# One x tile turned by DMA instead of TensorE, its loads behind it, the k-v copies first, five more stores at the end

## The chip, the cores and the metric

The kernel runs on one core of a Trainium2 chip. The metric is the device time of one execution in microseconds, as a median of several. Runs of the kernel before lie within 0.35 us of each other in any one set of rounds, about 0.1%. The second tool is the trace: the distances between the same two instructions on TensorE in two runs agree to some hundredths of a microsecond where nothing waits.

"Tile 6" below is the seventh group of 128 rows of x, counted from zero; "batch index 2" is the third of the eight batches. Group one is the second group of four tiles (4 to 7), group two the tiles 8 to 11. The prediction and the expectations count groups from one, so their "group two" is group one, and their "group three" is group two.

In the lines of the profile PE is TensorE, PEld its weight loads, DVE VectorE, ACT ScalarE, POOL GpSimd; a q behind a name (SPq) means that the engine's sequencer issues a DMA. L513 is line 513 of the kernel, and `out<-in` names the buffers written and read: xT is the turned x, raw_k the loaded k, ob an output tile on its way out. A line of a timeline gives start, length, what, and in brackets how long the engine was idle before and what ended that. The chain is the work that ended last, followed back from the end of the program; it shows start, length and what. A DMA "lands" when its completion semaphore has its full count.

## The reference, cut to what matters

```python
def _attn_ref(q, k, v):                      # batch 8, heads 8, rows 576, width 64
    q_p, k_p = phi(q, cos_w, sin_w), phi(k, cos_w, sin_w)     # relu, times cos and sin: width 128
    kv = np.einsum('bhsf,bhsd->bhfd', k_p, v)
    z = np.sum(k_p, axis=2)
    return np.einsum('bhsf,bhfd->bhsd', q_p, kv) / (np.einsum('bhsf,bhf->bhs', q_p, z)[..., None] + 1e-06)

def _moe_ref(x, w_gate, w_val, w_out):       # x: 4608 rows of 512, inner width 1536
    g = x @ w_gate
    return (g * (1.0 / (1.0 + np.exp(-g))) * (x @ w_val)) @ w_out
```

The result of the attention, rearranged to 4608 x 512, is the x of the second part.

## The kernel before

Nine groups of four x tiles go through the feed-forward part. While TensorE works on one group, the attention of the next is threaded into it: `at(step, ...)` puts small pieces of work behind the steps of the running group. A group has twelve steps of gate and value products (`ffn_fc`) and four output tiles (`ffn_out`); group zero's output is cut into twelve steps named (0, 0) to (2, 3).

A tile of x must be turned before the products can take it. There are two ways:

```python
def x_turn(t, fast=False):
    if fast:
        x_turn_pe(t)              # four transposes on TensorE, into PSUM
        x_turned(t, "act")        # a copy to xT on ScalarE
    else:
        nc.sync.dma_start_transpose(out=xT_of(t), in_=st["x", t])
```

The first product of a group takes all four tiles at once, so it waits for the last of the four turns:

```python
nc.tensor.matmul(out=..., lhsT=(wg_sb, wv_sb)[i][:, kc, fs], rhs=xT[tg][:, ts, kc], ...)   # L513
```

Loads of k and v are issued by GpSimd. To keep one back, the kernel lets GpSimd read two elements of something that a DMA writes:

```python
def load_2():
    nc.gpsimd.tensor_copy(out=hold2, in_=xT[1][0:1, 0, 0, 0:2])    # waits for tile 4's turn
    for nm in ("k", "v"):
        load(2, nm)

at((0, 1), turn(4), load_2)
at((1, 0), turn(5), a_(6, 0))
at((1, 1), a_(6, 1))
...
at((2, 0), turn(6, True))
at((2, 2), turn(7, True))
```

`load_3` does the same for batch index 3, held by tile 10. Where q of the second batch is turned, TensorE, ScalarE and VectorE meet:

```python
at("b11", lambda: kv_mm(1), q_(1, 0, 0), q_(1, 1, 0, "dve"), lambda: kv_out(1))
at((0, 0), lambda: kv_free(1), a_(4, 0), a_(4, 1))
```

`kv_mm` makes the k-v products, `q_` turns q on TensorE and copies it out (to phit), `kv_out` copies the k-v products out (to kvd), and `a_` multiplies the two. "b11" is the last product step of group zero.

## Time and profile before

| | before |
|---|---|
| time, median of 3 | 325.12 us |
| span in the trace | 323.2 us |
| TensorE busy | 316.1 us, 98% |
| VectorE, ScalarE, GpSimd busy | 56%, 40%, 11% |
| tile 5's transpose by DMA, issue to landing | 2.4 us |
| tile 10's, which holds the load of index 3 | 2.5 us |

With TensorE at 98% the question for any change is what TensorE no longer has to do, or no longer waits for. Busy time is not enough for that, since a wait of some tenths disappears in it; the start of the instruction behind the wait is the thing to read. The lines themselves are in the prediction.

### The profile page before, as it was taken

The page shows a single profiled execution, that of the slowest core. Times are in us where ns is not written, and L with a number is a line of the kernel's source. Part 1 is how long each engine was busy: PE and PEld are TensorE (multiplying, and loading weights), DVE is VectorE, ACT ScalarE, POOL GpSimd, SP SyncE. Part 2 cuts the span into 40 slices and gives each one's busy share as a digit, 9 for nine tenths or more (in the row PEclk, how much of TensorE's full clock was granted, in tenths as well). Part 3 has the DMA queues.
Part 4 walks back from the last instruction along what each step waited for, and adds up shares of the span by engine and source line. Part 5 has one row for each costly group of instructions (what it writes and reads, how often), then busy time and mean ns, then how long its engine had stood idle before and what let it go on. Part 6 is the DMA issues. An engine that isn't in the chain of part 4 may idle for free.

```text
span 323.2 us, 6031 instructions
## 1 busy us (share of the span) xinstructions
PE 316.1 (98%) x2384; PEld 159.0 (49%) x2384; DVE 180.9 (56%) x363; ACT 130.7 (40%) x239; POOL 35.3 (11%) x60
## 2 busy tenths in 40 slices
PE   7899999999999999999999999999999999999995
PEld 3596555454445444544454445444544444444443
DVE  7873766787448747564756555755573236323320
ACT  7553546662436345333533354335432132213311
POOL 6755002010101000110011000200000000000000
PEclk9999999999999999999999999999999999999999
DMA  7999997987995988599679968895912401240014
GB/s 267 215 200 197 206 194 136 213 113 108 178 200 79 184 152 134 79 175 177 116 97 160 164 123 118 134 184 109 134 36 48 103 14 35 50 103 11 0 32 97
DMA packets 74379, 41.01 MB, mean 127 GB/s; under 512 B 49904, under 2 KB 69104, under 8 KB 74352
## 3 DMA queue, kind: packets, MB, share of 16 engines
q1 hardware_dynamic: 52000, 22.95, 38.9%
q0 software_dynamic: 22192, 17.57, 36.6%
q8 instruction: 18, 0.29, 0.4%
q10 hardware_dynamic: 160, 0.13, 0.1%
q14 instruction: 9, 0.07, 0.1%
HBM read 37.75 MB, written 9.44 MB: 146 GB/s over the span
## 4 chain that ended last, share of the span: by engine, by line
PE 95%; ACT 2%; DVE 2%; issue 0%; ACTq 0%
PE banks L513 58%; PE banks L549 28%; PE banks L285 3%; PE banks L399 2%; PE banks L444 1%; PE banks L381 1%; DVE v L239 1%; PE banks L152 1%; PE banks L568 1%; PE banks L325 0%; PE banks L485 0%; ACT L184 0%; ACT phit L333 0%; PE banks L274 0%; ACT ob L571 0%; DVE qwT L369 0%
## 5 line engine op out<-in xcount | busy, mean ns | idle before, releaser
L524 DVE TENSOR_TENSOR ht<-sg,banks 128x512 bf16<-128x512 bf16 (+2 forms) x116 | 74.7, 650 | 68.7 <-PE banks L513 60.3
L513 PE MATMUL banks<-xT,wv_sb 128*128 128x512 bf16 (+2 forms) x464 | 111.3, 364 | 0.0
L513 PE MATMUL banks<-xT,wg_sb 128*128 128x512 bf16 (+2 forms) x464 | 111.3, 364 | 0.0
L519 ACT ACTIVATE sg<-banks 128x512 bf16<-128x512 f32 (+2 forms) x116 | 65.8, 568 | 111.6 <-PE banks L513 107.7
L549 PE MATMUL banks<-wo_sb,ht 128*128 128x512 bf16 x420 | 93.8, 379 | 0.0
L513 PEld LDWEIGHTS <-wv_sb 128*128 128x128 bf16 x464 | 44.8, 98 | 48.7
L513 PEld LDWEIGHTS <-wg_sb 128*128 128x128 bf16 x464 | 43.1, 98 | 42.8
L549 PEld LDWEIGHTS <-ht 128*128 128x128 bf16 x420 | 40.3, 98 | 45.7 <-issue 0.2
L556 ACT COPY ob<-banks 128x512 f32<-128x512 f32 x18 | 10.6, 586 | 54.0 <-PE banks L549 54.0
L235 DVE TENSOR_TENSOR r_q<-raw_q,tab 128x1152 bf16<-128x1152 bf16 x24 | 17.9, 754 | 20.7 <-ACT raw_q L218 20.7
L556 DVE COPY ob<-banks 128x512 f32<-128x512 f32 x17 | 11.7, 691 | 28.6 <-PE banks L549 28.6
L239 DVE TENSOR_TENSOR v<-raw_v,tab 128x1152 bf16<-128x1152 bf16 x31 | 22.8, 753 | 0.1
L421 DVE TENSOR_TENSOR x<-banks,rec 128x512 bf16<-128x512 f32 (+1 forms) x32 | 21.6, 674 | 1.3 <-PE banks L381 0.3
L218 ACT ACTIVATE raw_k<-raw_k 128x576 bf16<-128x576 bf16 (+1 forms) x25 | 17.1, 694 | 0.0
L218 ACT ACTIVATE raw_q<-raw_q 128x576 bf16<-128x576 bf16 x24 | 15.5, 679 | 0.0
L729 POOL COPY hold<-phit 1x2 bf16<-1x2 bf16 x5 | 0.9, 175 | 129.6 <-DMA phit<-r_q 129.6
L399 PEld LDWEIGHTS <-phit 128*128 128x128 bf16 (+1 forms) x240 | 10.0, 100 | 6.5 <-issue 1.3
L399 PE MATMUL banks<-kv,phit 128*128 128x65 bf16 (+1 forms) x240 | 11.6, 195 | 0.0
L152 PE MATMUL banks<-zeros 128*128 128x64 bf16 (+1 forms) x64 | 8.5, 292 | 1.0 <-DVE zeros L147 1.0
L308 DVE CAST kv<-banks 64x260 bf16<-64x260 f32 x12 | 5.1, 428 | 7.4 <-ACT kv L308 7.3
L285 PEld LDWEIGHTS <-raw_k 64*64 64x64 bf16 x504 | 7.6, 106 | 3.0 <-issue 2.1
L285 PE MATMUL banks<-v,raw_k 64*64 64x130 bf16 x504 | 8.8, 218 | 0.0
(84 smaller groups left out, 130.9 us busy)
## 6 DMA issues: line engine op xcount, KB each, us to landing
out_dram<-ob SPq DMA_DIRECT2D x70, 128.0 KB, 2.4
raw_k<-in_k_dram POOLq DMA_DIRECT2D x7, 576.0 KB, 9.1
raw_q<-in_q_dram POOLq DMA_DIRECT2D x6, 576.0 KB, 6.3
raw_v<-in_v_dram POOLq DMA_DIRECT2D x6, 576.0 KB, 12.0
wo_sb<-in_moe_w_out_dram POOLq DMA_DIRECT2D x3, 512.0 KB, 13.0
wg_sb<-in_moe_w_gate_dram POOLq DMA_DIRECT2D x5, 256.0 KB, 8.6
wv_sb<-in_moe_w_val_dram POOLq DMA_DIRECT2D x5, 256.0 KB, 9.2
wo_sb<-in_v_dram SPq DMA_DIRECT2D x2, 576.0 KB, 4.3
```

Of the source, the lines that this page charges most:

```text
L152: nc.tensor.matmul(out=ps, lhsT=zeros, rhs=zeros[:, 0:cols].unsqueeze(1).to_broadcast([P, 4, cols]), start=True, stop=True)
L218: nc.scalar.activation(out=out, in_=in_, func=AF.Relu)
L235: nc.vector.tensor_tensor(out=st[b, "q"][:, g], in0=o.unsqueeze(2).to_broadcast([P, NC, 2, D]), in1=tab, op=ALU.mult)
L239: nc.vector.tensor_tensor(out=v2s[b % 2][:, g, :, :, 0:D], in0=(first if b == 0 and g == 0 else {"v": raw_of(b, "v")})["v"][:, g].unsqueez ...
L285: nc.tensor.matmul(out=ps[i * D:(i + 1) * D, e, j * 2 * D1:(j + 1) * 2 * D1], lhsT=raws[b, "k"][es, g, c], rhs=v2s[b % 2][es, g, c, :, 0:D ...
L399: nc.tensor.matmul(out=ps[ms, e, g * D1:(g + 1) * D1], lhsT=phit[b][:, e, g, c:c + n].rearrange("p c s -> p (c s)"), rhs=kv2s[b % 2][:, e, ...
L421: nc.vector.tensor_tensor(out=st["x", t].rearrange("p (y e d) -> p e y d", e=2, d=D)[:, :, ys], in0=ps[:, :, 0:2 * J * D1].rearrange("p e ...
L513: nc.tensor.matmul(out=st["f", tg, fc, lo][i], lhsT=(wg_sb, wv_sb)[i][:, kc, fs], rhs=xT[tg][:, ts, kc], start=(kc == 0), stop=(kc == KC - 1))
L519: nc.scalar.activation(out=sg[:, 0:n], in_=st["f", tg, fc, lo][0], func=AF.Silu)
L524: nc.vector.tensor_tensor(out=hts[tg % 2][:, fc, r:r + n], in0=st.pop(("s", tg, fc, lo))[:, 0:n], in1=ps[1], op=ALU.mult)
L549: nc.tensor.matmul(out=o_ps[t], lhsT=hts[tg % 2][:, fc, r:r + P], rhs=wo_sb[:, fc], start=(fc == 0), stop=(fc == FC - 1))
L556: (nc.scalar.copy if t % 2 == 0 else nc.vector.tensor_copy)(out=ob, in_=ps)
```

## The change

Its intent: take four transposes and a copy off the engines, remove a small wait for kvd, give the loads and the attention of batches index 2 and 3 one more step of room, and arrange the last stores differently. Its core, with cuts marked:

```diff
-            nc.sync.dma_start(out=out_v[...], in_=ob[e * SH:(e + 1) * SH])
+            parts = 2 if NH - 9 <= idx < NH - 4 else 1
+            for i in range(parts):
+                cols = slice(i * d_model // parts, (i + 1) * d_model // parts)
+                nc.sync.dma_start(out=out_v[...][:, cols], in_=ob[e * SH:(e + 1) * SH, cols])
...
-                (nc.sync if e else nc.scalar).dma_start(out=out_v[...][:, lo:hi],
+                (nc.scalar if e else nc.sync).dma_start(out=out_v[...][:, lo:hi],
...
-    at("b11", lambda: kv_mm(1), q_(1, 0, 0), q_(1, 1, 0, "dve"), lambda: kv_out(1))
+    at("b11", lambda: kv_mm(1), lambda: kv_out(1), q_(1, 0, 0), q_(1, 1, 0, "dve"))
...
-        nc.gpsimd.tensor_copy(out=hold2, in_=xT[1][0:1, 0, 0, 0:2])
+        nc.gpsimd.tensor_copy(out=hold2, in_=xT[1][0:1, 1, 0, 0:2])
...
-    at((0, 1), turn(4), load_2)
+    at((0, 1), turn(4))
...
-    at((1, 1), a_(6, 1))
+    at((1, 1), a_(6, 1), turn(6), load_2)
...
-    at((2, 0), turn(6, True))
...                                  (k, v and q work of index 2 and 3: one step later each)
-            at((9, 10, 11)[i - 1] + SLOTS, lambda t=t: a_tile2(t), turn(t))
+            at((10, 11, 12)[i - 1] + SLOTS, lambda t=t: a_tile2(t), turn(t))
             if i == 2:
-                at(11 + SLOTS, load_3)
+                at(12 + SLOTS, load_3)
```

More of the change, by code (lines that the diff above doesn't have):

```diff
@@ L558, in ffn_out @@
             idx = 2 * t + e
-            nc.sync.dma_start(out=out_v[idx // NC, idx % NC], in_=ob[e * SH:(e + 1) * SH])
+            parts = 2 if NH - 9 <= idx < NH - 4 else 1
+            for i in range(parts):
+                cols = slice(i * d_model // parts, (i + 1) * d_model // parts)
+                nc.sync.dma_start(out=out_v[idx // NC, idx % NC][:, cols], in_=ob[e * SH:(e + 1) * SH, cols])
     def ffn_out_last(t):
@@ L573, in ffn_out_last @@
                 idx = 2 * t + e
-                (nc.sync if e else nc.scalar).dma_start(out=out_v[idx // NC, idx % NC][:, lo:hi],
+                (nc.scalar if e else nc.sync).dma_start(out=out_v[idx // NC, idx % NC][:, lo:hi],
                                                         in_=ob[e * SH:(e + 1) * SH, 0:hi - lo])
@@ L749 @@
         if b == 2:
-            fs, tq = [s0 + i for i in (0, 0, 1, 1, 4, 5, 5, 6)], (s0 + 2, s0 + 2)
+            fs, tq = [s0 + i for i in (0, 0, 1, 1, 5, 6, 6, 7)], (s0 + 4, s0 + 4)
         else:
@@ L754 @@
             if b == 3:
-                fs, tq = [p0 + 12 + i for i in range(4)] + [s0 + 4, s0 + 4, s0 + 5, s0 + 5], (s0 + 2, s0 + 2)
-            at(p0 + 3 if b < 5 else p0 + 1, lambda b=b: load_behind(b))
-        tk = (s0 + 4, s0 + {2: 8, 3: 7}.get(b, 5))
+                fs, tq = [p0 + 13 + i for i in range(4)] + [s0 + 5, s0 + 5, s0 + 6, s0 + 7], (s0 + 3, s0 + 3)
+            at(p0 + 4 if b < 5 else p0 + 1, lambda b=b: load_behind(b))
+        tk = (s0 + 4, s0 + {2: 9, 3: 8}.get(b, 5))
         for s, f in zip(fs, steps):
```

## The prediction

> **What bounds the kernel now.** I read the page first: the busy shares and the slices, then the chain that ended last.
>
> ```profile
> PE 316.1 (98%) x2384; PEld 159.0 (49%) x2384; DVE 180.9 (56%) x363; ACT 130.7 (40%) x239; POOL 35.3 (11%) x60
> ...
> PE   7899999999999999999999999999999999999995
> ...
> DMA  7999997987995988599679968895912401240014
> ...
> PE 95%; ACT 2%; DVE 2%; issue 0%; ACTq 0%
> ```
>
> TensorE is busy for 316.1 of 323.2 us, and the only slices of the forty under 9 are the first two and the last. The chain is 95% PE. So time comes out of this kernel only where TensorE issues less, or where it waits: at the head (not touched by the change), at the tail, and in small waits inside the slices that print as 9.
>
> A busy digit can hide such waits, because ends of matmuls are modelled. So I read the chain in order of time from 34 to 60 us, the stretch that most of the change touches; start, length, what:
>
> ```profile
> 38.88 1.27 PE banks L285 x69
> 40.15 0.51 PE banks L274 x7
> 40.66 0.02 issue
> 40.69 0.91 ACT phit L333
> 41.59 0.27 ACT kvd L297
> 41.87 0.01 issue
> 41.88 0.38 ACT kvd L297
> 42.26 0.04 issue
> 42.30 0.72 PE banks L444 x7
> ...
> 51.42 0.22 PE banks L485 x4
> 51.64 0.86 PE banks L549 x4
> ```
>
> Two things are to be seen. From 40.69 to 42.30 the chain leaves PE: ScalarE first copies the turned q (phit, 0.91 us), then two pieces of the k-v products (kvd), and only then the x products (L444) go on. And at 51.42 TensorE's four transposes of one x tile take 0.22 us of the chain.
>
> How much of the 1.6 us does TensorE really lose? The timeline of that stretch:
>
> ```profile
> 40.88 1.03 PE L549 MATMUL banks<-wo_sb,ht 128*128 128x512 bf16 x4
> 41.08 0.63 DVE L333 COPY phit<-banks 128x896 bf16<-128x896 bf16 x1 [0.77 <-PE banks L274]
> 41.49 0.76 ACT L297 CAST kvd<-banks 64x260 bf16<-64x260 f32 x2
> 41.62 0.86 DVE L297 CAST kvd<-banks 64x260 bf16<-64x260 f32 x2
> ...
> 41.83 0.30 PE L444 MATMUL banks<-kvd,phit 128*64 128x260 bf16 x1
> 42.30 0.45 PEld L444 LDWEIGHTS <-phit 128*64 128x64 bf16 x7 [0.36 <-ACT kvd L297]
> 42.30 0.72 PE L444 MATMUL banks<-kvd,phit 128*64 128x260 bf16 x7 [0.17 <-ACT kvd L297]
> ```
>
> Four output products fill most of the gap. The first of eight x products starts at 41.83, the second at 42.30. They step by about 0.11 us elsewhere (two of them are 0.22 us of the chain at 44.85), so 0.47 - 0.11 = 0.36 us is lost; the weight load's own 0.36 us before it agrees. The 0.17 us on the matmul line is the same wait less the modelled tail.
>
> In the rest of the kernel PE has no listed wait over 0.1 us from 56 to 112 us, and the chain from there is PE piece after PE piece. The end, in the chain and the timeline:
>
> ```profile
> 316.60 1.64 PE banks L568 x12
> ...
> 318.26 0.43 ACT ob L571
> ...
> 318.72 0.56 ACTq L574
> ...
> 319.40 0.32 ACT ob L571
> ```
>
> After 319.72 only the last two stores and the close of the program remain, to 323.2.
>
> [...]the slice with the 0.36 us stall prints as 9. So I count starts, not busy time. [...]the trace shows the pair, four L485 matmuls and a ScalarE copy to xT of 0.59 us. [...]the transposes of x by DMA land in 2.4 us where nothing else runs and in up to 10.5 us where loads do. So moving a transpose to DMA is free only in a quiet window. [...]here 128 KB stores land in 2.3 us and 48 KB ones in 1.9 to 2.1, so halving stores will shorten little.
>
> **The change part by part.**
>
> 1. k-v products of batch two copied out first (the second batch of eight). Both engines now copy kvd before phit. ScalarE is free at 39.35, the products end at 40.15; two copies of 0.38 end near 40.96, phit takes 0.91 more and ends near 41.87. VectorE is free at 40.31, copies kvd in 0.86 to 41.17 and phit in 0.63 to 41.80. The second x product needs ScalarE's kvd and phit: ready near 41.9 instead of 42.26, and it would come at 41.83 + 0.11 = 41.94 without a wait. The stall goes: -0.36 us, on the path.
>
> 2. x of tile 6 by DMA. Four transposes go: -0.22 us on the chain. ScalarE's 0.59 us copy goes too, off the path. The order of instructions confirms it: the first FFN product of the second group now waits for three DMA semaphores where it waited for two. x of tile 6 is finished on VectorE at 50.67 (49.91 + 0.76), -0.36 by step 1 = 50.31. A transpose in the quiet window there takes 2.4 us (the one of tile 5, issued at 48.44, landed so; the one at 45.50 took 4.4[...]). Landing near 52.7; needed by the weight load at 54.30 - 0.58 = 53.7. About 1 us of slack: no cost, if the load stays out.
>
> 3. That is what "k and v of batch three behind it" does (index 2): the load waits for tile 5's transpose rather than tile 4's. Released at 48.44 - 0.36 + 2.4 = 50.5 instead of 49.95, so 0.5 us later; before, its bytes began to flow about 2 us after issue (the DMA share of the windows table is 0.46 and 0.49 in 48 to 50 and 50 to 52, and 0.93 in 52 to 54). Now this is from about 53, after tile 6. k landed after 7.2 us, v after 11.1, so near 58 and 63; the first ReLU of k moves from fc 4 to fc 5 of the group (62.98 to about 64.4). Cost 0.
>
> 4. Everything of batches index 2 and 3 one step later. No work is added. For index 2 the copy-out of k-v and the first x products that need it stay one step apart, as they were; there the eight L399 products took 0.52 instead of 0.42, waiting 0.23 on the weight load for VectorE's copy, about 0.1 us. For index 3 the gap shrinks from two steps to one: the chain from the end of the products to the last copy is 103.60 to 105.34 = 1.74 us, an FFN step 8 x 0.216 = 1.73 us. So index 3 gets the same 0.1 us: +0.1 us.
>
> 5. x of tile 11 moves behind the first output tile, near 80.2. Its chain on VectorE (0.16 + 0.20 + 0.69, den at first waiting for PE) ends near 81.3, the transpose goes out behind two stores at 81.9, and group three needs it at 88.0 - 0.6 = 87.4. Slack 5.5 us less 2.4 for landing: 0, even with the k and v load beside it.
>
> 6. Five more stores. SyncE issues at about 0.55 to 0.59 us each. Tile 32's four: 312.04 + 4 x 0.57 = 314.3, before tile 33 is ready at 314.74. Tile 33's four: to 317.05, before tile 34 at 317.22. Then two to 318.4, before the last copy at 318.69. Margins of 0.2 to 0.4 us, no delay. The swap of SyncE and ScalarE for the last halves leaves one issue on each: 0, perhaps 0.1 either way.
>
> Sum: -0.36 - 0.22 + 0.10 = -0.48 us. 325.12 - 0.48 = 324.64; I say 324.6.
>
> **The rivals.** (a) The DMA transpose of tile 6 takes the place of the PE wait: with 4.4 us, as at 45.50, it lands at 54.7 and TensorE waits 1.0 us, so the time stays at about 325.6. For it: the slack is only 1 us and the stores queue on the same SyncE. Against it: in program order the transpose stands before all eight stores of the first group, the weights have landed by then, and the load waits. Chance 15%. (b) Tile 11's transpose meets k and v of index 3. Transposes beside loads took 6.9 us in the window 106 to 112, and that would still land at 88.8, 1.4 us late: 326.0. For it: the load is now released at nearly the same time (82). Against it: its bytes come about 2 us later. Chance 8%. (c) The tail: the five stores and the swap shift which earlier store each of the last ones waits for. If this shortens the close of the program, which takes 3.5 us after the last copy, it gives 0.2 to 0.5 us: 324.2. If issue of half stores is slower than I think, the last store goes out 0.5 us late: 325.1. (d) The removed waits are hidden anyhow: a later wait of PE absorbs them. Nothing speaks for it, since no engine but PE is on the chain from 43 to 318 us.
>
> **Range and chances.** All steps are tenths of a microsecond on a PE stream that cannot shrink. The rivals span 324.0 to 326.0, the runs of before lie within 0.3 us. 8 in 10: 323.9 to 325.3. 2% would be 6.5 us, more than ten times the sum of the saved parts; a loss of that size would need a deadline missed by 6 us in several places. Faster 0.01, same 0.98, slower 0.01.
>
> **What would show each step.** Step 1: the second L444 product of tile 4 follows the first by about 0.11 us, and no wait on kvd is listed; wrong, if it waits for phit instead. Step 2: 20 L485 products instead of 24, 31 DMA transposes of x instead of 30, and the first L513 of group two starts about 0.6 us earlier (53.9); wrong, if a wait on the xT DMA stands there. Step 3: k and v issued near 50.9. Step 4: the first eight or sixteen L399 products after the k-v products of index 3 show a wait on VectorE of 0.1 to 0.2. Step 5: no gap at the first L513 of group three. Step 6: 75 whole and half stores from L562 and the last copy still about 0.2 us behind TensorE's last product. The prediction fails as a whole if PE's idle time grows by over 0.5 us anywhere, or if the tail after the last copy differs from 3.5 us by over 0.3.

(The 4.4 us of the transpose at 45.50: the trace shows the last weights landed at 45.50, and loads of q still moving, which landed at 46.25 and 49.27.)

## The result, and the profile after

The changed kernel took 325.24 us (median of 4, 324.86 to 325.57), the kernel before in the same rounds 324.99 (324.85 to 325.15). A ratio here is the one of the fast runs of both kernels in the same rounds, and not quite the ratio of the medians; it is 1.0007, with a 95% interval of 0.999 to 1.0025. Whether the change costs or gains a few tenths is not settled by the times. The spread of the changed kernel is more than twice that of before, which is a first hint at something that does not happen alike in each run.

The page of the changed kernel, with the busy shares and the chain by engine and line:

```profile
PE 316.3 (98%) x2369; PEld 158.8 (49%) x2380; DVE 180.9 (56%) x363; ACT 130.3 (40%) x238; POOL 35.1 (11%) x60
...
PE 88%; DMA 5%; DVE 3%; ACT 2%; issue 0%; SPq 0%; ACTq 0%
PE banks L513 58%; PE banks L549 22%; DMA xT<-x 3%; PE banks L285 3%; PE banks L399 2%; DMA out_dram<-ob 1%; PE banks L381 1%; DVE v L239 1%; PE banks L152 1%; PE banks L444 0%; DVE x L469 0%; PE banks L325 0%; DVE num L455 0%; ACT L184 0%; ACT ob L556 0%
```

The busy time says nothing (316.3 against 316.1; some matmul records are missing, so the counts are not to be compared). The chain does: PE had 95% of it and now has 88%, and a line that was not there, "DMA xT<-x", has 3%. Something now waits for a transpose. (The chain counts a transpose over its whole length, so these shares are not lost time; how long TensorE waits follows below.)

The chain from 34 to 60 us shows the gain and the first loss:

```profile
39.94 0.38 ACT kvd L297
40.31 0.01 issue
40.33 0.37 ACT kvd L297
40.70 0.02 issue
40.72 0.91 ACT phit L333
41.63 0.04 issue
41.68 0.63 PE banks L444 x8
...
49.20 0.76 DVE x L469 x2
49.96 0.03 DVE num L455
49.99 3.94 DMA xT<-x
53.93 0.05 issue
53.98 6.22 PE banks L513 x28
```

kvd comes first, phit follows, and all eight L444 products run in one piece. But at 49.99 the transpose of tile 6 goes out and takes 3.94 us, and the first L513 of group one starts when it lands. The same in the timeline, with what GpSimd does in the meantime:

```profile
49.99 1.19 SPq L497 DMA_TRANSPOSE xT<-x  x1
50.22 0.17 POOL L707 COPY hold<-xT 1x2 bf16<-1x2 bf16 x1 [15.76 <-DMA xT<-x]
...
50.45 0.74 POOL L102 DMA_DIRECT2D raw_k<-in_k_dram  x1
...
53.97 0.55 PEld L513 LDWEIGHTS <-wg_sb 128*128 128x128 bf16 x4 [0.67 <-DMA xT<-x]
```

The load of k is released by tile 5's landing, 0.46 us after tile 6's transpose was issued, and not after it had landed. The second loss is at the next border between groups, in the chain from 76 to 90 us:

```profile
79.83 0.59 ACT ob L556
80.43 0.02 issue
80.44 0.47 SPq L562
80.91 0.05 issue
80.96 0.59 SPq L562
...
81.64 6.64 DMA xT<-x
88.28 0.05 issue
88.33 1.69 PE banks L513 x7
```

Tile 11's transpose stands behind an output copy and two stores, and then takes 6.64 us. TensorE's weight load waits 1.00 us for it. The load of k of index 3 was issued at 81.86, 0.22 us behind the transpose:

```profile
81.86 0.74 POOL L102 DMA_DIRECT2D raw_k<-in_k_dram  x1 [0.34 <-issue]
...
88.33 0.55 PEld L513 LDWEIGHTS <-wg_sb 128*128 128x128 bf16 x4 [1.00 <-DMA xT<-x]
```

In the kernel before neither wait exists; at both borders the first L513 follows the output products:

```profile
53.65 1.03 PE L549 MATMUL banks<-wo_sb,ht 128*128 128x512 bf16 x4
54.51 1.03 PE L513 MATMUL banks<-xT,wg_sb 128*128 128x512 bf16 x4
...
77.83 10.52 PE L549 MATMUL banks<-wo_sb,ht 128*128 128x512 bf16 x48
88.19 1.03 PE L513 MATMUL banks<-xT,wg_sb 128*128 128x512 bf16 x4
```

To see what each stretch of TensorE's work took, I take the start of four instructions in each run: the k-v products of batch index 1, the second output piece after them, the first L513 of groups one and two; and the end of the last product. The head (before the k-v products) differs by up to 0.4 us between runs of whatever kernel, so it is left out. In us:

| stretch on TensorE | before | changed |
|---|---|---|
| k-v products to the second output piece | 4.14 | 3.70 |
| from there to the first L513 of group one | 11.56 | 11.74 |
| to the first L513 of group two | 33.68 | 34.35 |
| to the end of the last product | 231.03 | 231.04 |
| sum | 280.41 | 280.83 |
| from there to the end of the span | 3.98 | 3.73 |

So 0.44 us is gained in the first stretch, 0.18 and 0.67 us are lost in the next two, and 0.25 us is gained after the last product. The sum is +0.17 us, near the +0.23 us that the ratio of 1.0007 stands for. (One traced run of each kernel; the span is printed to 0.1 us, so whatever is measured to its end, here and below, is good to 0.05 us.)

### The profile page after: what moved, and what is told of

The parts are those of the page before. It is cut to its first block, busy times and chain, and to the rows that moved or that the text cites. A ratio compares the mean times of both kernels' runs of the same rounds, so it can differ in the third digit from the quotient of the medians.

```text
span 323.1 us, 6021 instructions
## 1 busy us (share of the span) xinstructions
PE 316.3 (98%) x2369; PEld 158.8 (49%) x2380; DVE 180.9 (56%) x363; ACT 130.3 (40%) x238; POOL 35.1 (11%) x60
## 4 chain that ended last, share of the span: by engine, by line
PE 88%; DMA 5%; DVE 3%; ACT 2%; issue 0%; SPq 0%; ACTq 0%
PE banks L513 58%; PE banks L549 22%; DMA xT<-x 3%; PE banks L285 3%; PE banks L399 2%; DMA out_dram<-ob 1%; PE banks L381 1%; DVE v L239 1%; PE banks L152 1%; PE banks L444 0%; DVE x L469 0%; PE banks L325 0%; DVE num L455 0%; ACT L184 0%; ACT ob L556 0%
## 5 line engine op out<-in xcount | busy, mean ns | idle before, releaser
L513 PE MATMUL banks<-xT,wg_sb 128*128 128x512 bf16 (+2 forms) x464 | 111.3, 364 | 0.7 <-DMA xT<-x 0.7
L513 PE MATMUL banks<-xT,wv_sb 128*128 128x512 bf16 (+2 forms) x464 | 111.3, 364 | 0.0
L513 PEld LDWEIGHTS <-wv_sb 128*128 128x128 bf16 x464 | 44.8, 98 | 48.7
L513 PEld LDWEIGHTS <-wg_sb 128*128 128x128 bf16 x464 | 43.0, 98 | 44.2 <-DMA xT<-x 1.7
L152 PE MATMUL banks<-zeros 128*128 128x64 bf16 (+1 forms) x64 | 9.4, 309 | 1.0 <-DVE zeros L147 1.0
```

The lines of the kernel that those rows point to most:

```text
L152: nc.tensor.matmul(out=ps, lhsT=zeros, rhs=zeros[:, 0:cols].unsqueeze(1).to_broadcast([P, 4, cols]), start=True, stop=True)
L513: nc.tensor.matmul(out=st["f", tg, fc, lo][i], lhsT=(wg_sb, wv_sb)[i][:, kc, fs], rhs=xT[tg][:, ts, kc], start=(kc == 0), stop=(kc == KC - 1))
```

## The experiments

The theory after reading the trace: the two gains of the prediction are real, and they are given back because the two transposes meet a load that is issued within half a microsecond of them. The rivals: the gain of the reorder was absorbed anyhow; the stores, not the loads, slow the transposes; the shift of the batches as a whole holds group two.

### The reorder alone

```diff
 # on the kernel before
-    at("b11", lambda: kv_mm(1), q_(1, 0, 0), q_(1, 1, 0, "dve"), lambda: kv_out(1))
+    at("b11", lambda: kv_mm(1), lambda: kv_out(1), q_(1, 0, 0), q_(1, 1, 0, "dve"))
```

> The kernel before with the copy-out of the k-v products alone moved ahead of the turned q. Theory (the change gains 0.45 us here and 0.2 us by the transposes taken off TensorE, and gives it back at two waits for a DMA transpose of x at the starts of groups two and three): 0.35 to 0.5 us faster than before, about 324.55; the second L444 product follows the first at once, no wait on kvd listed, and no wait of TensorE on xT anywhere. Rival (the reorder is worth nothing, the next wait absorbs it): 0 to 0.1 us faster.

Measured: 324.46 us (5 runs) against 324.78, ratio 0.9989 (0.9975 to 1.0002). The interval just touches 1, the stretches do not leave a doubt: 3.71 us instead of 4.14 in the first, every other one as before (11.56, 33.68), so 0.43 us is gained and nothing absorbs it. TensorE in the timeline of this run:

```profile
41.01 1.03 PE L549 MATMUL banks<-wo_sb,ht 128*128 128x512 bf16 x4
42.08 0.64 PE L444 MATMUL banks<-kvd,phit 128*64 128x260 bf16 x8
42.65 0.61 PE L549 MATMUL banks<-wo_sb,ht 128*128 128x512 bf16 x2
```

The eight products follow without the break that the lines of before show at 41.83 and 42.30. There is no wait on xT in this run.

### The loads held until the transpose has landed

Three kernels, all from the changed one: the load of index 2 held for tile 6, the load of index 3 held for tile 11, and both.

```diff
 # b_load6 and d_both, in load_2
-        nc.gpsimd.tensor_copy(out=hold2, in_=xT[1][0:1, 1, 0, 0:2])
+        nc.gpsimd.tensor_copy(out=hold2, in_=xT[1][0:1, 2, 0, 0:2])
 # c_load11 and d_both, in load_3, which moves behind tile 11's turn
-        nc.gpsimd.tensor_copy(out=hold2, in_=xT[2][0:1, 2, 0, 0:2])
+        nc.gpsimd.tensor_copy(out=hold2, in_=xT[2][0:1, 3, 0, 0:2])
-            if i == 2:
+            if i == 3:
```

> The changed kernel, but k and v of batch index 2 are held until tile 6's transpose has landed, not tile 5's. Theory, in the form that these loads slow the transpose: it lands in about 2.4 us instead of 3.9, TensorE's wait at the first L513 of group two (0.67 us on the weight load) goes, and the time falls by 0.4 us against the changed kernel. Rival (the stores of the first group, or something else than the loads, slow it): still 3.5 to 4 us, wait and time as in the changed kernel.

> The changed kernel, but k and v of batch index 3 are held until tile 11's transpose has landed, not tile 10's. Theory: that transpose lands in about 2.5 us instead of 6.6, TensorE's wait at the first L513 of group three (1.00 us on the weight load) goes, and the time falls by 0.65 us against the changed kernel. Rival (stores slow it, or the wait moves to the later k and v): landing 5 us or more, or a new wait of TensorE for the k-v products of index 3, time as in the changed kernel.

> Both holds together. Theory: no wait of TensorE on xT is left, 1.0 to 1.1 us faster than the changed kernel, about 324.2, and 0.7 to 0.9 under the kernel before. Rival (the two waits overlap with something else that ends as late): less than 0.4 us faster than the changed kernel.

| | time (5 runs) | ratio to before (95%) | tile 6 lands after | tile 11 | to group one | to group two |
|---|---|---|---|---|---|---|
| before | 324.78 | | on TensorE | 2.4 | 11.56 | 33.68 |
| hold for 6 | 324.04 | 0.9983 (0.997 to 0.9995) | 2.4 | 2.4 | 11.39 | 33.68 |
| hold for 11 | 324.49 | 0.9989 (0.9977 to 1.0002) | 3.8 | 2.4 | 11.61 | 33.68 |
| both | 324.06 | 0.9976 (0.9964 to 0.9989) | 2.4 | 2.5 | 11.38 | 33.68 |

Each hold brings its own transpose to 2.4 or 2.5 us and takes its own wait away. The stores were not moved, so they are not what slows the transposes: with the hold for 6, two stores follow tile 6's transpose at 1.29 and 1.90 us as they do without it, and with the hold for 11 the same two stores still stand ahead of tile 11's. With both holds the kernel takes 324.06 us, 0.7 us under before in the same rounds; the theory's form with numbers said about 324.2.

One thing was not expected: holding only tile 6's load also freed tile 11. The timeline of that run tells why:

```profile
81.92 1.25 SPq L497 DMA_TRANSPOSE xT<-x  x1
82.18 0.17 POOL L742 COPY hold<-xT 1x2 bf16<-1x2 bf16 x1 [7.68 <-DMA xT<-x]
...
82.70 0.74 POOL L102 DMA_DIRECT2D raw_k<-in_k_dram  x1 [0.34 <-issue]
```

Here tile 10, which releases the load, happened to land later, and k of index 3 went out 0.78 us behind tile 11's transpose instead of 0.22. That was enough. What delayed tile 10 was not tested; its transpose landed in 3.5 us, beside a load of q issued at 73.77 (71.92 in the changed kernel). One of the five runs took 324.88 us, so tile 11 may not be freed in each of them; that run was not traced.

### The DMA transpose alone, with the load where it was

```diff
 # on the kernel before; load_2 stays held by tile 4
-    at((1, 1), a_(6, 1))
+    at((1, 1), a_(6, 1), turn(6))
-    at((2, 0), turn(6, True))
```

> The kernel before with tile 6 turned by DMA alone; k and v of batch index 2 stay released by tile 4. Theory (loads issued before or within half a microsecond of a transpose slow it): they are issued about 0.4 us ahead of it, it lands in 5 to 8 us, TensorE waits 2 to 4 us at the first L513 of group two, and the time rises by 2 to 3.5 us over before. Rival (the half microsecond of delay of the loads does not matter): landing about 4 us, wait under 0.7, time within 0.5 us of before.

Measured: 332.67 us (4 runs, 328.75 to 332.77) against 324.85, ratio 1.0202 (1.0139 to 1.0265; unclear, since 2% lies inside the interval). Both the theory and the rival undershot: the transpose, issued at 50.55 behind a load issued at 49.88, took 8.9 us. TensorE in the timeline, and the granted clock (the number before the last two) in a table of windows of the same run:

```profile
59.52 1.89 PE L513 MATMUL banks<-xT,wg_sb 128*128 128x512 bf16 x4 [5.17 <-DMA xT<-x]
61.20 1.91 PE L513 MATMUL banks<-xT,wv_sb 128*128 128x512 bf16 x4
62.91 1.91 PE L513 MATMUL banks<-xT,wg_sb 128*128 128x512 bf16 x4
64.61 1.10 PE L513 MATMUL banks<-xT,wv_sb 128*128 128x512 bf16 x4
65.55 1.03 PE L513 MATMUL banks<-xT,wg_sb 128*128 128x512 bf16 x4
```

```profile
54.00:59.50 5.50, 0.35 (x2) 0.00 (x0) 0.69 (x1) 0.11 (x1) 0.00 (x0) 0.86 1.19 224
59.50:62.00 2.50, 2.48 (x6) 0.89 (x7) 0.00 (x0) 0.55 (x2) 0.00 (x0) 0.50 0.79 298
62.00:64.00 2.00, 2.00 (x6) 0.76 (x5) 0.78 (x2) 1.19 (x3) 0.00 (x0) 0.50 0.00 0
```

The wait itself makes the stretch to group one 16.71 us instead of 11.56, which is 5.15 us. Then twelve products run at half speed, with a granted clock of 0.50, and the stretch to group two is 36.25 instead of 33.68, another 2.57 us. Together 7.7 of the 7.8 us. So the half of the change that looked like bookkeeping, "k and v behind it", is what keeps the DMA transpose from costing 2%. The one run of 328.75 us lost 3.9 us, less than the wait alone in the traced run. Its mean clock, 0.994, lies between the 0.990 of the other three and the 0.997 to 1.000 of the kernel before, so it probably had a shorter wait and a shorter slow stretch; its trace was not taken.

In this run the granted clock falls to 0.50 at 57.93, 3.6 us after the last product before the wait, and is back at 1.00 at 64.75, 5.2 us after the products resumed. What sets these two times was not tested. The waits of up to 1.00 us in the changed kernel leave its clock at 1.00.

### Tile 11's products moved back

```diff
 # on the changed kernel
-            at((10, 11, 12)[i - 1] + SLOTS, lambda t=t: a_tile2(t), turn(t))
+            at((10, 11, 11)[i - 1] + SLOTS, lambda t=t: a_tile2(t), turn(t))
```

> The changed kernel with the x products of tile 11 moved back ahead of the first output tile (beside tile 10's, one FFN step after tile 9's). Theory: its transpose goes out at about 79.5, before the load is released, lands in about 2.5 us; no wait at the first L513 of group three; 0.65 us faster than the changed kernel, the wait at group two stays. Rival (the delay of the whole batch is what holds group three): the 1.00 us wait stays.

Measured: 324.39 us (4 runs) against 324.85, ratio 0.9985 (0.9971 to 1.0000). Tile 11's transpose goes out at 80.46 and lands in 2.4 us, 1.76 us before the load's issue; the stretch to group two is 33.69, the wait is gone, and the one at group one stays (0.9 us on the weight load). So it is not the delay of the whole batch that holds group two but the place of this one transpose, behind two stores and beside a load. The stretch to group two gains 0.66 us, as expected (0.65). By medians of different rounds the gain is 0.85 us (325.24 less 324.39), but the changed kernel's own runs spread by 0.7.

### How close is too close

Every run holds one or two of these pairs. The time from the issue of the transpose to the issue of the load of k that follows, against the landing of the transpose:

| load of k after transpose (us) | transpose lands after (us) | which |
|---|---|---|
| -0.67 | 8.9 | tile 6, load held by tile 4 |
| +0.22 to +0.23 | 6.0 to 6.8 | tile 11, in the changed kernel and four of its variants |
| +0.46 to +0.49 | 3.8 to 4.2 | tile 6, in the changed kernel and five variants |
| +0.78 | 2.4 | tile 11, hold for 6 |
| +0.94 | 2.4 | tile 6, without the stores |
| +1.08 to +1.26 | 2.4 | tile 11, in the kernel before, the reorder alone, the transpose alone and before with five stores |
| +1.7 and more | 2.4 to 2.5 | the holds, and tile 11 moved back |

Within each of the two places the order is the same, so it is not the place. In these runs a load issued 0.8 us or more behind such a transpose left it alone.

The DMA packets in the traces show what meets what. A transpose that lands in 2.4 us moves its 512 packets of 256 bytes between 1.2 and 2.0 us after its issue, and 32 small ones follow at once. In these pairs the first packet of the load of k moves 1.4 to 1.7 us after the load's issue. In the changed kernel that is 2.07 us after the issue of tile 6's transpose: all 512 packets were through, but the 32 small ones moved only 3.05 to 3.61 us after the issue. At tile 11 it is 1.87 us, with 130 of the 512 still to go; with the load held by tile 4 it is 0.78 us, before the first of them. In every pair that landed in 2.4 or 2.5 us, the load's first packet came 2.2 us or later.

### The end: stores, swap, and what remains open

The changed kernel is 0.25 us shorter after the last product. Five kernels look at that, each the changed kernel with one thing different, save the last:

```diff
 # g_nostores
-            parts = 2 if NH - 9 <= idx < NH - 4 else 1
+            parts = 1
 # m_six: NH - 10 <= idx;   n_three: NH - 7 <= idx
 # k_noswap
-                (nc.scalar if e else nc.sync).dma_start(
+                (nc.sync if e else nc.scalar).dma_start(
 # i_stores: the kernel before with the five more stores alone
```

> The changed kernel without the five more stores. The tail from the last product's end to the end of the span was 3.98 us in before, 3.99 in the reorder alone, 3.73 in the changed kernel. The last two stores take turns on eight completion semaphores: numbers 0 and 1 in before, 6 and 7 in the changed kernel, here 1 and 2. Theory (SyncE's closing waits go through the eight in order, and what stands behind the last one that fires costs about 0.04 us each): tail 3.90 to 3.97 here. Rival one (smaller stores finish sooner): 3.98 again too, so the run with six tells. Rival two (the swap of the issuing engines shortens it): 3.72.

> The changed kernel with six more stores instead of five (one more in the tile before). The last two stores then use semaphores 7 and 0. Theory (place in a row of closing waits): the saving of 0.25 us goes, tail 3.95 to 4.05, or near 3.75 if the store on number 7 happens to be the last to land. Rival (more and smaller stores shorten the tail): 3.72 or less. Rival (swap): 3.72.

> The changed kernel with the swap of the last issues undone. From the last ScalarE issue to the end of the span: before 3.45 us, the changed kernel 3.15, without the stores 3.54, with six 3.64. If the swap matters: near 3.45. If only the stores do: 3.05 to 3.20.

> The changed kernel with three more stores instead of five; the last two stores use semaphores 4 and 5. Issue to end: if smaller stores shorten the end, between 3.15 and 3.54; if it is the place in a row of closing waits, 3.2 to 3.35; if it is something that only happens at 6 and 7, 3.45 or more.

> The kernel before with the five more stores alone; the last two stores use semaphores 5 and 6, one off the changed kernel's. Issue to end: if the five small stores are the cause, 3.05 to 3.20; if the semaphore numbers are, 3.2 or more.

The order of the built instructions shows on which of eight completion semaphores, used in turn, the last two stores lie. From ScalarE's last issue to the end of the span, in us:

| kernel | more stores | last two on | issue to end | last product to end |
|---|---|---|---|---|
| before; reorder alone | 0 | 0 and 1 | 3.45; 3.46 | 3.98; 3.99 |
| transpose alone; without the stores | 0 | 1 and 2 | 3.57; 3.54 | 4.10; 4.08 |
| three | 3 | 4 and 5 | 3.65 | 4.18 |
| before with five | 5 | 5 and 6 | 3.66 | 4.25 |
| changed; both holds; without the swap | 5 | 6 and 7 | 3.15; 3.10; 3.17 | 3.73; 3.69; 3.76 |
| six | 6 | 7 and 0 | 3.64 | 4.22 |

The swap does nothing. Smaller stores do nothing either: five of them on the kernel before make the end 0.27 us longer, six in the changed kernel make it 0.5 us longer. (From the unrounded spans in the traces these are 0.21 and 0.46 us.) What goes with the short end is that the last two stores lie on numbers 6 and 7, in every run that has it. My own theory was a row of closing waits in which what stands behind the last store costs 0.04 us each. It asks for a steady fall from 0 to 7, and 1, 4 and 5 are longer than 0, so alone it does not do.

The traces hold SyncE's closing waits one by one, which no view shown here lists, and they show that the theory had hold of a part. The last landing comes 2.10 to 2.13 us after the last issue in all these runs, and SyncE then goes through the eight numbers in order, about 0.06 us each. In the kernel before, the last landing is number 0's; seven more waits follow it, until 2.56 us after the issue. In the changed kernel it is number 6's, and one follows, until 2.22 us. That difference of 0.34 us is the whole gain (0.33 us from issue to end, unrounded). In the other kernels a further pause stands among the closing instructions: 0.11 us in those on 1 and 2, 0.44 in those on 4 and 5 and on 5 and 6, 0.31 in the one on 7 and 0. Taken off, it leaves ends of 3.46, 3.43, 3.24, 3.17 and 3.13 us for pairs that begin with 0, 1, 4, 5 and 6, which is the steady fall. What the pause is stays open. So in the changed kernel a gain of about 0.25 us hangs on the count of all stores and transposes before the end.

The times of these kernels (324.85 and 325.33 for the first two, 325.13, 325.20 and 325.02) are not fit to judge a quarter of a microsecond, since most of them carry the waits for transposes too: the runs of the first two differ among themselves by 1.3 and 1.7 us.

### A version that beats both

The load of index 2 held for tile 6, and tile 11's products back in their place:

```diff
 # on the changed kernel
-        nc.gpsimd.tensor_copy(out=hold2, in_=xT[1][0:1, 1, 0, 0:2])
+        nc.gpsimd.tensor_copy(out=hold2, in_=xT[1][0:1, 2, 0, 0:2])
-            at((10, 11, 12)[i - 1] + SLOTS, lambda t=t: a_tile2(t), turn(t))
+            at((10, 11, 11)[i - 1] + SLOTS, lambda t=t: a_tile2(t), turn(t))
```

> A version meant to beat both: the changed kernel with the load of batch index 2 held for tile 6 and tile 11's products moved back ahead of the first output tile. Theory: neither transpose meets a load, no wait of TensorE on xT, time as with both holds, 324.0 to 324.2, 0.2 to 0.25% under before. Rival (one of the two still waits sometimes): medians of 324.3 or more and a spread of over 0.5 us.

Measured: 324.07 us (5 runs, 323.91 to 324.17) against 324.83, ratio 0.9975 (0.9962 to 0.9989). No wait on xT is listed. TensorE at the two borders in its timeline:

```profile
52.85 1.03 PE L549 MATMUL banks<-wo_sb,ht 128*128 128x512 bf16 x4
53.72 1.03 PE L513 MATMUL banks<-xT,wg_sb 128*128 128x512 bf16 x4
```

```profile
86.31 1.24 PE L549 MATMUL banks<-wo_sb,ht 128*128 128x512 bf16 x5
87.39 1.03 PE L513 MATMUL banks<-xT,wg_sb 128*128 128x512 bf16 x4
```

At both borders five or four output products at 0.216 us each are followed by the L513 without a gap, and the spread of the times is about a third of the changed kernel's (0.26 against 0.71 us). The sum from the k-v products to the last product is 279.80 us against 280.41, and the end 3.68 against 3.98.

## Why the prediction was right or wrong

The class (within 2%) and the range were right: 325.24 lies inside 323.9 to 325.3, at its upper edge. The number was not: a gain of 0.48 us was worked out, and none came. That the time stayed inside the range is partly luck: without the 0.25 us at the end, which the prediction's sum did not contain, it would have been 325.49. And by its own last signs the prediction failed: TensorE waited longer than the 0.5 us named there (1.00 us on one weight load), and the end after the last copy was 3.2 us, over 0.3 from 3.5 (3.16 unrounded). By its steps:

1. k-v products first, -0.36 us: right, and a little small. The first stretch gave 0.44 us in the changed kernel and 0.43 alone.
2. Tile 6 by DMA: the part on TensorE is right in kind; without the wait the stretch to group one shrank by 0.17 us (11.56 to 11.39), where 0.22 was put. (An L485 transpose shows as 0.22 us in the trace; taking four of them away shortened the stream by about 0.04 us each.) But "Landing near 52.7; needed by the weight load at 54.30 - 0.58 = 53.7. About 1 us of slack: no cost" is wrong: it landed at 53.93.
3. The cause is the step "k and v of batch three behind it", of which the prediction said: "Now this is from about 53, after tile 6. ... Cost 0." The load went out at 50.45, near the 50.5 for its release, and its bytes did not stay out of the transpose's way: 3.9 us instead of 2.4. Two microseconds of grace after an issue were assumed from the DMA share in a table of windows two microseconds wide; a table that coarse cannot show when a transfer begins to matter. The load's first packet moved 1.60 us after its issue, at 52.05, and the transpose's last ones were not through. This was rival (a), at 15%, with a smaller cost than put there (0.35 us, by 11.74 against 11.39, instead of 1.0). But (a) gave the stores on SyncE as its ground and counted the load as held off, so it had the wait and not its cause.
4. One step of spacing for index 3, +0.10 us: did not happen. Apart from the borders no stretch is longer (231.03 and 231.04 after group two's start, which holds these products).
5. Tile 11, "Slack 5.5 us less 2.4 for landing: 0, even with the k and v load beside it": wrong, and the largest error. The issue was foreseen well (81.9, it came at 81.64) and so was the load's release (82; 81.86). The landing took 6.6 us, close to the 6.9 us that rival (b) named at 8%. Its two times decide the matter: the deadline at 87.4 less 81.64 leaves 5.8 us, and 6.6 us is more. The cost was 0.67 us.
6. The stores delayed nothing, as said; but the end shortened by 0.25 us, which rival (c) had as a possibility, with another mechanism (which earlier store each of the last ones waits for). The traces put it in the order of SyncE's closing waits (about 0.06 us each; seven behind the last landing before, one after).

The sum of what was measured: -0.44 - 0.17 + 0.35 + 0.67 - 0.25 = +0.16 us, where the prediction had -0.36 - 0.22 + 0.10 = -0.48. So the gains were right within 0.1 us each, and the difference is the two transposes, less the end. Both waits had been listed as rivals, the second with its cause, and were left out of the number because a load "issued" was taken for a load "not yet there". Rival (d), gains absorbed by a later wait, fell with the reorder alone.

Two readings of the prediction need a correction. That the slice with the 0.36 us stall prints as 9 says little about busy time: the slice is 8.1 us long, and would print as 9 with 0.8 us idle. And a loss of 2% did not need "a deadline missed by 6 us in several places": in the run with the transpose alone one missed by 5.2 us was enough, because the clock fell too (0.50 from 57.93 to 64.75).

## What to carry to other kernels

A transpose moved from TensorE to DMA has a deadline where the next group of products starts. Compare it with the landing that the same transfer has beside a load (3.8 to 8.9 us here), not with the one in a quiet window (2.4 us), if a load may be issued close to it (here 0.49 us behind it was too close, and 0.78 us was not); and hold the load on the landing of that very transpose, not of the one before. On a kernel at 98% of one engine, measure parts by distances between instructions on that engine: the times alone would have said "no effect" of a change that gained 0.6 us, lost 1.0 us in two waits and gained 0.25 us at the end.
